# Start-up of a fused convolution and gated-MLP kernel: unbroken TensorE warm-up, held weight requests, one scaling moved to GpSimd

## Chip, cores, metric

One core of one Trainium2 chip. The metric is the device time in microseconds (us) of one execution, the median of several. A profile is one more execution, taken with the hardware profiler; its span is about 1.7 us shorter than the device time of the same execution.

## The reference

```python
def _attn_ref(x, weight):                  # x (8, 4096, 192), weight (8 heads, 7 taps)
    w = softmax of weight over the taps
    x_pad = six zero tokens before each sequence
    out = for each token, head: sum over 7 taps of w[head, k] * x_pad[token + k]
def _moe_ref(x, w_in, w_out, beta):        # 32768 tokens, w_in (192, 2048), w_out (2048, 192)
    h = x @ w_in
    g = h * (1.0 / (1.0 + np.exp(-beta * h)))
    return g @ w_out
```

## The kernel before

Tokens go through in 32 chunks, each of two times 512 tokens. A chunk is a causal 7-tap convolution (`ct`), then 16 units of `hidden` (six matmuls into PSUM, then one Silu on ScalarE) and, interleaved, the output matmuls of `g` with `w_out`. The prediction calls one row-packed couple of output matmuls a pair, and unit u of chunk s is the step (s, u). A request lands when the last of its DMA engines has reported; the drain is the end of the kernel, when little more than output matmuls is left; the clock is released when TensorE's matmuls, throttled at first, go over to their full pace (here from one every 427 ns to one every 231).

Only the start differs from the steady loop. Chunk 0 is transposed on TensorE, its convolution runs mostly as matmuls with diagonal weights, and everything that the loop needs must arrive meanwhile: x, `w_in` in four parts (each part in two requests from GpSimd, which also cast to bf16), and `w_out` in four parts (from the SP queue, scaled by 1/beta afterwards).

```python
    load_x(x0, 0)                       # SP queue, in this order
    load_x(x1, TOK)
    for i in range(NW - 1):
        load_w_out(i)
    load(2)
    load_w_out(NW - 1)
    load(3)
    ...
    load_w_in(0)                        # GpSimd queue, two requests, at 2.2 us
    ...
    def fill(n, cols=TOK):              # matmuls of zeros that only keep TensorE busy
        for _ in range(n):
            nc.tensor.matmul(
                pf[:, 0, 0:cols], zeros[:, 0:128], zeros[:, 0:cols], start=True, stop=True
            )
    ...
    fill(5)
    pc = in_a()
    pw, pb = pc[:, 0, 0 : K + 1], pc[:, 1, 0:NF]
    nc.tensor.matmul(                   # tap weights onto 128 partitions
        pw, sel.rearrange("i h p -> i (h p)"), e8, start=True, stop=True
    )
    fill(1, 384)
    for b in range(NB):
        cast_rows(nc.vector.tensor_copy, x0b, x0, b)
    ...
    hold = setup.tile([1, 1], BF16)
    nc.gpsimd.tensor_copy(hold, x0b[0:1, 0, 0, 0, 0:1])   # waits for the first cast
    for i in range(1, NW):
        load_w_in(i)                    # the other six requests
    ...
    for b in range(NB):
        transposes(pt, x0b, b)
        nc.scalar.copy(tokens(xt0, b), pt)
        # fills of 256, 384, 384 columns, beta's transpose, 256 columns
    ...
    # chunk 0's convolution: 7 + 7 + 2 matmuls of N=512 ("conv matmuls"), 5 taps on VectorE
    nc.vector.reciprocal(beta_r, beta)
    scale_w_out(0)                      # VectorE
    ...
    CONV1 = {4: (0, 2), 5: (2, 4), 6: (4, 6), 7: (6, K)}  # chunk 1's third on TensorE, by unit
    QUOTA_A = {3: 4, 7: 2}              # output pairs in units up to 7 of chunk 0
```

Of the kernel before, what the change touches and what calls it, by code (L numbers as in the profile page):

```python
# [9 lines left out]
FP32 = mybir.dt.float32  # L10
FP32R = mybir.dt.float32r
BF16 = mybir.dt.bfloat16
# [5 lines left out]
def kernel(  # L18
# [17 lines left out]
    nc = tc.nc  # L36

    B, S, D = x.shape
    H, K = weight.shape
# [5 lines left out]
    TOK = 512  # L45
    NF = F // 128
    PAD = K - 1
    HALO = 16
# [13 lines left out]
    setup = ctx.enter_context(tc.tile_pool(name="setup", bufs=1))  # L62
# [18 lines left out]
    def in_a():  # L81
        return psum_a.tile([128, 2, TOK], FP32, name="pa")
# [20 lines left out]
    def cast(ch, h):  # L103
        if h == 0:
            xbs[ch] = xb_pool.tile([128, NB, NG, 2, DG], BF16, name="xb")
        nc.vector.tensor_copy(  # L106
            xbs[ch][:, :, :, h, :],
            xfs[ch][:, h].rearrange("q b (p c) -> q b c p", c=NG),
        )
# [13 lines left out]
    def xpose(ch):  # L123
        xt = new_xt(ch)
        halo(ch, xts[ch - 1])
        for b in range(NB):
            nc.sync.dma_start_transpose(
                xt[:, :, HALO + b * BLK : HALO + (b + 1) * BLK],
                xbs[ch][:, b].rearrange("q c h p -> q (c h p)"),
            )  # L130


    NW = 4
# [4 lines left out]
    x0b = setup.tile([128, NB, NG, 2, DG], BF16)  # L138
# [11 lines left out]
    e8 = setup.tile([H, K + 1], FP32)  # L150
# [18 lines left out]
    for i in range(NW - 1):  # L169
# [2 lines left out]
    load_w_out(NW - 1)  # L172
    load(3)

    zeros = setup.tile([128, TOK], BF16)
    nc.vector.memset(zeros, 0.0)
    warm = setup.tile([H, 1], FP32)
    nc.vector.memset(warm, 0.0)  # L178
    xt0 = setup.tile([128, NG, HALO + TOK], FP32R)
# [3 lines left out]
    sel = setup.tile([H, 2, DG], FP32)  # L183
# [6 lines left out]
        fill=0.0,  # L190
# [8 lines left out]
        fill=0.0,  # L199
# [7 lines left out]
    def load_w_in(i):  # L207
        cols = slice(i * FW, (i + 1) * FW)
        for r in range(2):
            nc.gpsimd.dma_start(  # L210
                out=w_in_s[r * DG : (r + 1) * DG, :, cols], in_=w_in_v[:, :, cols]
            )

    load_w_in(0)

    nmax = setup.tile([H, 1], FP32)
    nc.vector.reduce_max(nmax, cw8, axis=mybir.AxisListType.X, negate=True)
    nc.scalar.activation(
        e8[:, 0:K], cw8, AF.Exp, bias=nmax, accum_out=e8[:, K : K + 1]
    )  # L220
    nc.scalar.activation(warm, warm, AF.Silu)
    ident_b = setup.tile([128, 128], BF16)
    nc.vector.tensor_copy(ident_b, ident)
    pf = psum_h.tile([128, 2, TOK], FP32, name="ph")

    def fill(n, cols=TOK):
        for _ in range(n):
            nc.tensor.matmul(  # L228
                pf[:, 0, 0:cols], zeros[:, 0:128], zeros[:, 0:cols], start=True, stop=True
            )  # L230

    def cast_rows(copy, xb, x, b):
        copy(  # L233
            xb[:, b].rearrange("q c h p -> q h c p"),
            x[:, b // 2, :, b % 2].rearrange("q h (p c) -> q h c p", c=NG),
        )

    def transposes(pt, xb, b):
        for c in range(NG):
            nc.tensor.transpose(  # L240
                pt[:, c, :], xb[:, b, c].rearrange("q h p -> q (h p)"), ident_b
            )

    def tokens(xt, b):
        t = HALO + (b // 2) * 2 * BLK
        return xt[:, :, t : t + 2 * BLK].rearrange("p c (q b) -> p c b q", b=2)[:, :, b % 2]
# [2 lines left out]
    beta_r = setup.tile([128, NF], FP32)  # L249
    cw = consts.tile([128, K], FP32)  # L250
    rn = setup.tile([128, 1], FP32)

    fill(5)
    pc = in_a()
    pw, pb = pc[:, 0, 0 : K + 1], pc[:, 1, 0:NF]
    nc.tensor.matmul(
        pw, sel.rearrange("i h p -> i (h p)"), e8, start=True, stop=True
    )
    fill(1, 384)
    for b in range(NB):  # L260
        cast_rows(nc.vector.tensor_copy, x0b, x0, b)
    nc.vector.reciprocal(rn, pw[:, K : K + 1])
    nc.vector.tensor_scalar_mul(cw, pw[:, 0:K], rn)

    hold = setup.tile([1, 1], BF16)
    nc.gpsimd.tensor_copy(hold, x0b[0:1, 0, 0, 0, 0:1])
    for i in range(1, NW):
        load_w_in(i)

    diag = setup.tile([128, K, 128], FP32R)  # L270
    xt1 = setup.tile([128, HALO + TOK], FP32R)
# [19 lines left out]
    for b in range(NB):  # L291
        pt = pts[b % 2][:, b // 2, 0 : NG * BLK].rearrange("p (c q) -> p c q", c=NG)
        transposes(pt, x0b, b)
        nc.scalar.copy(tokens(xt0, b), pt)
        if b == 0:
            fill(1, 256)
        elif b == 1:
            fill(1, 384)
    fill(1, 384)
    nc.tensor.transpose(pb, beta_q, ident[0:NF, 0:NF])  # L300
    nc.scalar.copy(beta, pb)
    fill(1, 256)
    for k0, k1 in ((0, 3), (3, K)):
        nc.vector.tensor_tensor(
            diag[:, k0:k1],
# [4 lines left out]

    def scale_w_out(i):
        fcs = slice(i * NQ, (i + 1) * NQ)
        nc.vector.tensor_tensor(  # L313
            w_out_s[:, fcs, :],
            w_out_raw[:, fcs, :],
            beta_r[:, fcs].unsqueeze(2).to_broadcast((128, NQ, D)),
            ALU.mult,
        )
# [28 lines left out]
    nc.vector.tensor_tensor(dst, pv, dst, ALU.add)  # L347
    nc.vector.reciprocal(beta_r, beta)
    scale_w_out(0)


# [25 lines left out]
        nc.vector.tensor_copy(xt1[:, HALO - PAD :], xt[:, 0, HALO - PAD :])  # L377


    CONV1 = {4: (0, 2), 5: (2, 4), 6: (4, 6), 7: (6, K)}  # L380
    conv1_ps = []

    def conv1(u):
        if not conv1_ps:
            new_ct(1)
            conv1_ps.append(in_b())
        pv = conv1_ps[0]
        for k in range(*CONV1[u]):
            for r in range(2):
                diag_tap(k, xt1, pv[:, r, :], slice(r * DG, (r + 1) * DG))  # L390
# [7 lines left out]
    def conv_ops(s, c0):  # L398
        def op(k):
            if s not in cts:  # L400
                new_ct(s)
            o = HALO - PAD + k
            tap(cts[s][:, c0:, :], xts[s][:, c0:, o : o + TOK], k)

        return [lambda k=k: op(k) for k in range(K)]
# [82 lines left out]
    def jobs_of(s):  # L488
        for h in range(2):
            for q in range(0, NB, 2):  # L490
                if s == N_ST - 1 and h == 1 and q == NB - 2:
                    waiting.extend([Job(s, h, q, 1), Job(s, h, q + 1, 1)])
                else:
                    waiting.append(Job(s, h, q, 2))

    def output(s, u, pairs, free):
        for _ in range(pairs):
            for name in free:
                if slots[name] is None and waiting:
                    slots[name] = waiting.popleft()  # L500

            live = [(j.s, j.h, j.q, n) for n, j in slots.items() if j is not None]
            for *_, name in sorted(live):
                job = slots[name]
                if job.ready(s, u):
                    break
            else:
                return
            if job.po is None:
                job.po = place[name]()  # L510
            if job.pair():
                job.leave()
                slots[name] = None

    def rows_of(ch):
        for h in range(2):
            cast(ch, h)
        xpose(ch)


    first_work = {
        4: [None, lambda: scale_w_out(1), None],
        5: [None],
        7: [conv1_evac, lambda: scale_w_out(2), lambda: rows_of(2), None],
        8: [None, lambda: scale_w_out(3)],
        9: [None],
        10: [None],
    }

    QUOTA_A = {3: 4, 7: 2}  # L530
    queue = deque()
    for s in range(N_ST):
        jobs_of(s)
        for u in range(NF):
            if s > 0 or u > 1:
                hidden(s, u)
            elif u == 0:
                phs = [hidden(0, fc, [0]) for fc in range(2)]
                for j in range(1, NG):
                    for fc in range(2):  # L540
                        hidden(0, fc, [j], phs[fc])
                second()
            if s > 0:
                output(s, u, 8 if s < N_ST - 1 else 7, "ab")
            elif u > 7:
                output(s, u, 5 if u < NF - 1 else 8, "ab")
            elif u in QUOTA_A:
                output(s, u, QUOTA_A[u], "a")
            if s == 0:
                if u in CONV1:  # L550
                    conv1(u)
                if u == min(CONV1):
                    queue.extend(conv_ops(1, 1))
                for work in first_work.get(u, []):
                    (work or queue.popleft())()
            else:
                if u % 2 and queue:
                    queue.popleft()()

                if u == 0 and s + 3 < N_CH:  # L560
                    load(s + 3)
                if u < 2 and s + 2 < N_CH:
                    cast(s + 2, u)
                if u == 1 and s + 2 < N_CH:
                    xpose(s + 2)
            if u == 12 and s + 2 < N_CH:
                queue.extend(conv_ops(s + 2, 0))
# [32 lines left out]
```

## Time and profile before

| | before |
|---|---|
| device time, median | 693.09 us (692.62 to 693.2, 3 runs) |
| span of the profiled run | 690.7 us |
| first conv matmul | 7.83 us |
| first `hidden` matmul | 12.88 us |
| first Silu | 14.31 us |
| first Silu of chunk 1 | 32.57 us |

Read such a profile from its end: which chain of work ended last? This is part 4 of the page of the kernel before, by engine; by line its largest entries are `hidden` (L417, 47%) and the output matmuls (L450, 24% into each of two PSUM tiles). L279 is the conv matmul.

```profile
PE 97%; DVE 1%; ACT 1%; issue 0%; ACTq 0%
...
```

TensorE is full from 32 us to the drain, so a change of the start is worth exactly what it shifts the moment when TensorE becomes full, plus the work that is left for the end. The timeline of the kernel before, some lines (start us, duration us, engine, line, operation, output<-inputs, count, and in brackets the idle time before and what ended it):

```profile
7.83 3.04 PE L279 MATMUL ph<-xt,diag 128*128 128x512 f32 x7
...
10.71 1.79 PE L279 MATMUL pb<-xt,diag 128*128 128x512 f32 x7
...
12.88 1.47 PE L417 MATMUL ph<-ct,w_in_s 64*128 64x512 bf16 x12
...
14.31 16.15 ACT L425 ACTIVATE g<-ph,beta 128x1024 bf16<-128x1024 f32 x15
14.45 0.96 DVE L313 TENSOR_TENSOR w_out_s<-w_out_raw,beta_r 128x768 bf16<-128x768 f32 x1 [0.62 <-DMA w_out_raw<-in_moe_w_out_dram]
```

The first group of seven conv matmuls takes 3.04 us and the second 1.79, with the same operands: the TensorE clock is released in between (427 ns from start to start, then 231). The first scaling waits for `w_out`.

The chain of waits of the kernel before, for the window from 0 to 45 us, some lines (start us, duration us, what):

```profile
22.33 0.68 DVE ct L396
23.01 0.01 issue
23.02 0.69 DVE ct L396
23.72 0.03 issue
23.75 0.96 DVE w_out_s L313
24.71 1.20 DVE xb L106 x2
...
30.59 1.29 DVE ct L335
31.88 0.04 issue
31.92 0.61 PE ph L417 x4
```

The last obstacle before the steady loop is VectorE, which finishes chunk 1's taps at 31.88 us. What TensorE waited for in the first 36 us of the kernel before (total us, times, longest):

```profile
PE ph L228 <- DVE warm L178: 1.3, 1, 1.3
PE ph L417 <- ACT g L425: 0.9, 2, 0.7
PE ph L417 <- DVE ct L335: 0.4, 1, 0.4
PE pa L256 <- ACT e L218: 0.2, 1, 0.2
```

### The profile page before, as it was taken

The page shows a single profiled execution, that of the slowest core. Times are in us where ns is not written, and L with a number is a line of the kernel's source. Part 1 is how long each engine was busy: PE and PEld are TensorE (multiplying, and loading weights), DVE is VectorE, ACT ScalarE, POOL GpSimd, SP SyncE. Part 2 cuts the span into 40 slices and gives each one's busy share as a digit, 9 for nine tenths or more (in the row PEclk, how much of TensorE's full clock was granted, in tenths as well). Part 3 has the DMA queues.
Part 4 walks back from the last instruction along what each step waited for, and adds up shares of the span by engine and source line. Part 5 has one row for each costly group of instructions (what it writes and reads, how often), then busy time and mean ns, then how long its engine had stood idle before and what let it go on. Part 6 is the DMA issues. An engine that isn't in the chain of part 4 may idle for free.

```text
span 690.7 us, 24335 instructions
## 1 busy us (share of the span) xinstructions
PE 684.2 (99%) x11311; PEld 518.1 (75%) x11311; DVE 526.6 (76%) x466; ACT 579.1 (84%) x531; POOL 6.8 (1%) x18
## 2 busy tenths in 40 slices
PE   8999999999999999999999999999999999999997
PEld 4677777777777777777777777777777777777776
DVE  6888877797777797777887777887777977777712
ACT  6988888888888888888888888888888888888883
POOL 3000000000000000000000000000000000000000
DMA  9754332344332343332344332443323443322111
GB/s 214 176 117 116 93 104 69 85 116 112 92 104 58 102 116 104 97 95 61 109 116 105 93 83 70 116 116 92 104 56 98 116 106 98 98 60 60 48 37 59
DMA packets 121445, 66.86 MB, mean 97 GB/s; under 512 B 53232, under 2 KB 121344, under 8 KB 121344
## 3 DMA queue, kind: packets, MB, share of 16 engines
q1 hardware_dynamic: 119632, 63.73, 34.7%
q0 software_dynamic: 1664, 1.57, 1.4%
q8 instruction: 88, 1.44, 0.9%
q14 instruction: 13, 0.11, 0.1%
q10 hardware_dynamic: 48, 0.01, 0.0%
HBM read 29.89 MB, written 25.17 MB: 80 GB/s over the span
## 4 chain that ended last, share of the span: by engine, by line
PE 97%; DVE 1%; ACT 1%; issue 0%; ACTq 0%
PE ph L417 47%; PE pa L450 24%; PE pb L450 24%; DVE ct L335 1%; ACT g L425 0%; PE ph L279 0%; ACT x1b L233 0%; DVE w_out_s L313 0%; PE pb L279 0%; PE ph L228 0%; DVE ct L396 0%; DVE xb L106 0%; ACT ct L326 0%; PE pb L240 0%; PE ph L240 0%
## 5 line engine op out<-in xcount | busy, mean ns | idle before, releaser
L425 ACT ACTIVATE g<-ph,beta 128x1024 bf16<-128x1024 f32 x512 | 569.7, 1114 | 95.7 <-PE ph L417 89.6
L450 PEld LDWEIGHTS <-g 64*128 64x128 bf16 x8160 | 367.7, 94 | 106.3 <-ACT g L425 0.7
L417 PE MATMUL ph<-ct,w_in_s 64*128 64x512 bf16 x3072 | 422.8, 376 | 1.3 <-ACT g L425 0.9
L335 DVE SCALAR_TENSOR_TENSOR ct<-xt,cw,ct 128x1536 bf16<-128x1536 bf16 (+2 forms) x190 | 336.6, 1772 | 2.5
L450 PE MATMUL pa<-w_out_s,g 64*128 64x192 bf16 x4112 | 244.2, 243 | 0.6 <-ACT g L425 0.5
L450 PE MATMUL pb<-w_out_s,g 64*128 64x192 bf16 (+1 forms) x4048 | 229.7, 243 | 0.0
L417 PEld LDWEIGHTS <-w_in_s 64*128 64x128 bf16 x3072 | 156.7, 94 | 56.7 <-issue 3.4
L468 DVE TENSOR_REDUCE osb<-pa 128x384 f32<-128x768 f32 x64 | 61.3, 957 | 120.8 <-PE pa L450 119.9
L468 DVE TENSOR_REDUCE osb<-pb 128x384 f32<-128x768 f32 x63 | 60.3, 958 | 28.9 <-PE pb L450 28.8
L106 DVE CAST xb<-xf 128x768 bf16<-128x768 f32 x60 | 40.5, 677 | 0.0
L333 DVE TENSOR_SCALAR ct<-xt,cw 128x1536 bf16<-128x1536 bf16 (+2 forms) x32 | 31.1, 972 | 0.0
L466 ACT COPY osb<-pb 128x192 f32<-128x192 f32 x1 | 0.3, 318 | 6.7 <-PE pb L450 6.7
L228 PE MATMUL ph<-zeros 128*128 128x512 bf16 (+2 forms) x10 | 4.7, 551 | 1.3 <-DVE warm L178 1.3
L210 POOL DMA_DIRECT2D w_in_s<-in_moe_w_in_dram x8 | 5.2, 653 | 0.0
L279 PE MATMUL pb<-xt,diag 64*128 64x512 f32 (+1 forms) x21 | 4.7, 453 | 0.0
L313 DVE TENSOR_TENSOR w_out_s<-w_out_raw,beta_r 128x768 bf16<-128x768 f32 x4 | 3.8, 956 | 0.7 <-DMA w_out_raw<-in_moe_w_out_dram 0.6
L121 DVE COPY xt<-xt 128x18 bf16<-128x18 bf16 x27 | 4.3, 159 | 0.0
L326 ACT CAST ct<-ph 128x512 bf16<-128x512 f32 x1 | 0.6, 586 | 3.3 <-PE ph L279 3.3
L279 PEld LDWEIGHTS pb<-xt,diag 64*128 64x128 f32 (+1 forms) x21 | 2.7, 187 | 0.7
L279 PE MATMUL ph<-xt,diag 128*128 128x512 f32 x7 | 3.0, 603 | 0.1
L233 DVE CAST x0b<-x 128x384 bf16<-128x384 f32 x4 | 1.5, 420 | 2.1 <-DMA x<-in_x_dram 2.1
L228 PEld LDWEIGHTS <-zeros 128*128 128x128 bf16 x10 | 1.2, 133 | 2.1 <-DVE warm L178 1.3
(51 smaller groups left out, 27.7 us busy)
## 6 DMA issues: line engine op xcount, KB each, us to landing
out_dram<-osb SPq DMA_DIRECT2D x127, 192.0 KB, 2.1
xf<-in_x_dram SPq DMA_DIRECT2D x60, 384.0 KB, 4.1
xt<-xb SPq DMA_TRANSPOSE x120, 3.1
x<-in_x_dram SPq DMA_DIRECT2D x4, 384.0 KB, 4.6
w_in_s<-in_moe_w_in_dram POOLq DMA_DIRECT2D x8, 192.0 KB, 9.8
w_out_raw<-in_moe_w_out_dram SPq DMA_DIRECT2D x4, 384.0 KB, 14.6
out_dram<-osb SPq DMA_DIRECT2D x2, 96.0 KB, 1.6
cw<-in_weight_dram ACTq DMA_DIRECT2D x1, 0.2 KB
```

The lines of the kernel that those rows point to most:

```text
L106: nc.vector.tensor_copy(xbs[ch][:, :, :, h, :], xfs[ch][:, h].rearrange("q b (p c) -> q b c p", c=NG),)
L121: nc.vector.tensor_copy(dst, last[:, :, HALO + TOK - PAD :])
L210: nc.gpsimd.dma_start(out=w_in_s[r * DG : (r + 1) * DG, :, cols], in_=w_in_v[:, :, cols])
L228: nc.tensor.matmul(pf[:, 0, 0:cols], zeros[:, 0:128], zeros[:, 0:cols], start=True, stop=True)
L279: nc.tensor.matmul(pv, diag[rows, k, :], xt[rows, o : o + TOK], start=(k == k0), stop=(k == K - 1),)
L313: nc.vector.tensor_tensor(w_out_s[:, fcs, :], w_out_raw[:, fcs, :], beta_r[:, fcs].unsqueeze(2).to_broadcast((128, NQ, D)), ALU.mult,)
L333: nc.vector.tensor_scalar_mul(dst, src, scalar)
L335: nc.vector.scalar_tensor_tensor(out=dst, in0=src, scalar=scalar, in1=dst, op0=ALU.mult, op1=ALU.add)
L417: nc.tensor.matmul(ph[:, h, :], w_in_s[rows, j, fc * 128 : (fc + 1) * 128], cts[s][rows, j, :], start=(j == 0), stop=(j == NG - 1),)
L425: nc.scalar.activation(gs[s][:, fc], ph, AF.Silu, scale=beta[:, fc : fc + 1])
L450: nc.tensor.matmul(self.po[:, r, b * D : (b + 1) * D], g[rows, fc, self.h, q * BLK : (q + 1) * BLK], w_out_s[rows, fc, :], start=(self.don ...
L468: nc.vector.tensor_reduce(dst, self.po[:, :, 0 : nb * D].rearrange("p r n -> p n r"), axis=mybir.AxisListType.X, op=ALU.add,)
```

## The change

The intent: (1) keep TensorE busy with eight unbroken N=512 matmuls until the first transposes, so that the clock is released sooner, and do the tap weights' matmul later, among the transposes; (2) hold `w_in` back with two tiny GpSimd copies as barriers: chunk 0's part until ScalarE's Exp is done, the rest until chunk 0 is transposed, so that x and `w_out` come first; (3) put the first `w_out` scaling on GpSimd; (4) end chunk 1's TensorE part one unit earlier and shift output pairs into chunk 0 (52 instead of 49). Cut to its core:

```diff
-    load_w_in(0)
-
     nmax = setup.tile([H, 1], FP32)
     ...                                              # (Exp of the tap weights -> e8)
     nc.scalar.activation(warm, warm, AF.Silu)
+    hold = setup.tile([1, 2], FP32)
+    nc.gpsimd.tensor_copy(hold[:, 0:1], e8[0:1, K:])
+    load_w_in(0)
@@
-    fill(5)
     pc = in_a()
     pw, pb = pc[:, 0, 0 : K + 1], pc[:, 1, 0:NF]
-    nc.tensor.matmul(pw, sel..., e8, ...)
-    fill(1, 384)
+    fill(8)
     for b in range(NB):
         cast_rows(nc.vector.tensor_copy, x0b, x0, b)
-    (reciprocal, cw)
-    hold = setup.tile([1, 1], BF16)
-    nc.gpsimd.tensor_copy(hold, x0b[0:1, 0, 0, 0, 0:1])
-    for i in range(1, NW):
-        load_w_in(i)
@@ in the loop of transposes
         elif b == 1:
-            fill(1, 384)
-    fill(1, 384)
+            nc.tensor.matmul(pw, sel..., e8, ...)
+            (reciprocal, cw)
+            fill(1, 256)
+        elif b == 2:
+            fill(1, 256)
+    fill(1)
     nc.tensor.transpose(pb, beta_q, ident[0:NF, 0:NF])
+    fill(1)
     nc.scalar.copy(beta, pb)
-    fill(1, 256)
+    nc.gpsimd.tensor_copy(hold[:, 1:2], xt0[0:1, 0, HALO + TOK - 1 :].bitcast(FP32))
+    for i in range(1, NW):
+        load_w_in(i)
@@ scale_w_out(i)
-        nc.vector.tensor_tensor(
+        (nc.vector if i else nc.gpsimd).tensor_tensor(
@@
-    CONV1 = {4: (0, 2), 5: (2, 4), 6: (4, 6), 7: (6, K)}
+    CONV1 = {4: (0, 2), 5: (2, 4), 6: (4, K)}
-        7: [conv1_evac, lambda: scale_w_out(2), lambda: rows_of(2), None],
+        6: [conv1_evac, lambda: scale_w_out(2), lambda: rows_of(2), None],
-    QUOTA_A = {3: 4, 7: 2}
+    QUOTA_A = {4: 2, 7: 5}
-                output(s, u, 5 if u < NF - 1 else 8, "ab")
+                output(s, u, 5 if u < NF - 1 else 10, "ab")
```

Below, "first hold" is the barrier before chunk 0's `w_in`, "second hold" the later barrier before the other six requests.

More of the change, by code (lines that the diff above doesn't have):

```diff
@@ L173 @@
     load(3)
-    zeros = setup.tile([128, TOK], BF16)
+    zeros = setup.tile([128, 128], BF16)
     nc.vector.memset(zeros, 0.0)
@@ L226, in fill @@
     def fill(n, cols=TOK):
+        zc = zeros.unsqueeze(1).to_broadcast((128, cols // 128, 128))
         for _ in range(n):
-            nc.tensor.matmul(
-                pf[:, 0, 0:cols], zeros[:, 0:128], zeros[:, 0:cols], start=True, stop=True
-            )
+            nc.tensor.matmul(pf[:, 0, 0:cols], zeros, zc, start=True, stop=True)
     def cast_rows(copy, xb, x, b):
@@ L251 @@
     rn = setup.tile([128, 1], FP32)
-    fill(5)
     pc = in_a()
     pw, pb = pc[:, 0, 0 : K + 1], pc[:, 1, 0:NF]
-    nc.tensor.matmul(
-        pw, sel.rearrange("i h p -> i (h p)"), e8, start=True, stop=True
-    )
-    fill(1, 384)
+    fill(8)
     for b in range(NB):
         cast_rows(nc.vector.tensor_copy, x0b, x0, b)
-    nc.vector.reciprocal(rn, pw[:, K : K + 1])
-    nc.vector.tensor_scalar_mul(cw, pw[:, 0:K], rn)
-    hold = setup.tile([1, 1], BF16)
-    nc.gpsimd.tensor_copy(hold, x0b[0:1, 0, 0, 0, 0:1])
-    for i in range(1, NW):
-        load_w_in(i)
     diag = setup.tile([128, K, 128], FP32R)
@@ L297 @@
         elif b == 1:
-            fill(1, 384)
-    fill(1, 384)
+            nc.tensor.matmul(
+                pw, sel.rearrange("i h p -> i (h p)"), e8, start=True, stop=True
+            )
+            nc.vector.reciprocal(rn, pw[:, K : K + 1])
+            nc.vector.tensor_scalar_mul(cw, pw[:, 0:K], rn)
+            fill(1, 256)
+        elif b == 2:
+            fill(1, 256)
+    fill(1)
     nc.tensor.transpose(pb, beta_q, ident[0:NF, 0:NF])
+    fill(1)
     nc.scalar.copy(beta, pb)
-    fill(1, 256)
+    nc.gpsimd.tensor_copy(hold[:, 1:2], xt0[0:1, 0, HALO + TOK - 1 :].bitcast(FP32))
+    for i in range(1, NW):
+        load_w_in(i)
     for k0, k1 in ((0, 3), (3, K)):
```

## The prediction

> **What bounds the kernel now.** The chain that ended last is 97% TensorE (page, part 4); from 32 us to the drain no wait separates one matmul from the next, and nothing there changes. Gains must come before 32 us, or from work left for the end.
>
> From the timeline and the chain:
> - The clock is cold until about 10.2 us: N=512 matmuls start 427 ns apart, afterwards 231 ns apart. So the first conv group (L279, 7 matmuls, from 7.83) takes 2.9 us to issue, the second 1.6. The chain runs through that group, then ScalarE (0.59 conv copy, 1.32 x1b, 0.58, 1.32) to the first Silu at 14.31.
> - From there TensorE is nearly full (about 1.06 to 1.12 us per unit), with stalls of 0.75 and 0.18 (PSUM held by Silu), 0.4 near 29 us (the last w_out scaling on VectorE) and about 0.6 at 31.3, where chunk 1 waits for VectorE's last tap; the chain is VectorE from 22.3 to 31.9.
> - DMA: w_in is issued at 2.17 but its first packets move at 5.7, dividing the engines with x1 and w_out until 21 us. w_out part 0 lands at 14.36 (its scaling waits 0.6 us), part 1 at 18.2, when its scaling starts.
>
> **The change.**
> 1. Warm-up: eight N=512 fills, about 1.1 to 4.6 us, without the tap-weight matmul (0.49 us). The Trainium skill ("TensorE: Matmul & The Clock Gate", Part 1) gives a free-running activity window of about 3.4 us; Part 4 says that transposes do not count as busy. This trace agrees so far: fills broken by mixed work did not release the clock. One unbroken window may end the cold phase at 5 to 8 us. The fills after the transposes are longer (512+512 columns for 384+256), costing up to 0.5 us if cold. Warm, conv starts about 7.5 (after ScalarE's copies of xt0), its sixteen matmuls take 3.7 us, and the first Silu moves to about 13.1: -1.2 us. If the clock stays cold to 10 us: about 0.
> 2. w_in held: chunk 0's starts about 1.7 us later, but x1 is then done; I estimate that it lands by 11 us (before 12.0). w_out and the loads of chunk 2 land 1 to 4 us earlier.
> 3. The first scaling leaves VectorE: -0.96 us on its chain. On GpSimd I estimate 1.7 us (skill, "GPSIMD Engine Reference", section 3.1: 2.6 cycles per element with two inputs, 768 elements), off the path.
> 4. conv1 ends one unit earlier, so its evacuation starts earlier. The last tap of chunk 1 ends near 30.2 (before 31.88).
> 5. Chunk 0 takes 52 output pairs instead of 49: three pairs of 82 ns leave the drain, -0.25 us.
>
> **Sum:** chunk 1 starts 1.0 to 1.8 us earlier, plus 0.25. Prediction **691.4 us**, 690.3 to 692.7. Faster by over 2%: 1%; within 2%: 98.5%; slower: 0.5%.
>
> **What would show each step.** Conv matmuls 231 ns apart from the first or second one (step 1). First Silu near 13.1. w_in chunk 0 landed before hidden starts; w_out scalings without DMA waits. GpSimd scaling 1.5 to 2.2 us, ended before the first output matmul. ct of chunk 1 ready near 30.2; waits at 29 and 31.5 us shrunk to under 0.3.
>
> **What would make it wrong.** A window phase that keeps the clock cold into conv (gain about 0.5); w_in for chunk 0 landing after 11.5 us; a GpSimd scaling over 3 us; a new wait for chunk 2's loads before its casts.

## More of the kernel before

The queues of the kernel before from 11 to 14 us (packets, MB, share of the time of 16 engines; q0 carries `w_in`, q1 the SP queue's loads), and after them the time from issue to landing of the eight `w_in` requests:

```profile
q0 software_dynamic: 415, 0.39, 77.2%
q1 hardware_dynamic: 415, 0.31, 40.7%
```

```profile
DMA to landing us min/median/max: 8.3/9.8/13.0
```

The two queues moved the same number of packets, 415 each. The Trainium skill says the same in "DMA: Bandwidth & Descriptors", section "Queues, rings and completion order": each DMA engine takes the queues that have work in turn, packet by packet. This trace agrees from 7 to 19 us: in each microsecond the two counts differ by at most 4 (where `w_in`'s queue held only the rest of one request they were far apart, 188 and 761 from 11 to 14 us in the changed kernel). So `w_in` gets every second packet while `w_out` and x are waiting, however urgent it is.

## The result, and the profile after

694.12 us median (693.69 to 694.41, 4 runs) against 693.0 (692.62 to 693.2, 4 runs): ratio 1.0016, interval 0.9999 to 1.0034. The predicted range, 690.3 to 692.7, does not hold it.

| us | before | changed |
|---|---|---|
| first conv matmul | 7.83 | 8.40 |
| clock released | about 10.4 | about 9.9 |
| second request of chunk 0's `w_in` landed | 12.00 | 15.05 |
| first `hidden` that needs it | 12.88 | 15.09 |
| first Silu | 14.31 | 16.44 |
| first Silu of chunk 1 | 32.57 | 34.77 |
| span | 690.7 | 692.7 |

What TensorE waited for in the first 36 us of the changed kernel (L422 is `hidden` now, L272 the conv matmul, L234 the fills):

```profile
PE ph L422 <- DMA w_in_s<-in_moe_w_in_dram: 1.6, 1, 1.6
PE ph L422 <- ACT g L430: 1.1, 3, 0.7
PE ph L234 <- DVE warm L178: 1.1, 1, 1.1
PE pb L244 <- DVE x0b L237: 0.4, 1, 0.4
```

The first line is new. Its place in the changed kernel's timeline, TensorE and ScalarE lines:

```profile
8.40 2.69 PE L272 MATMUL ph<-xt,diag 128*128 128x512 f32 x7
...
10.93 1.77 PE L272 MATMUL pb<-xt,diag 128*128 128x512 f32 x7
...
13.09 0.39 PE L422 MATMUL ph<-ct,w_in_s 64*128 64x512 bf16 x1
...
15.09 1.25 PE L422 MATMUL ph<-ct,w_in_s 64*128 64x512 bf16 x10 [1.61 <-DMA w_in_s<-in_moe_w_in_dram]
...
16.44 1.11 ACT L430 ACTIVATE g<-ph,beta 128x1024 bf16<-128x1024 f32 x1 [1.83 <-PE ph L422]
```

One matmul goes (it needs the first request's 64 partitions only), then TensorE stands until the second request has landed. The chain of waits of the changed kernel, window 0 to 45 us, runs through a later part of the same weights and names the barrier:

```profile
7.82 0.51 ACT xt L287
8.33 0.05 issue
8.39 0.17 POOL hold L304
8.56 0.57 POOL w_in_s L210
9.13 10.98 DMA w_in_s<-in_moe_w_in_dram
20.11 0.05 issue
20.15 0.69 PE ph L422 x5
```

That is the second hold: part 1 of `w_in`, issued at 8.5 us, landed at 20.11 and held up unit 4 as well. The `w_in` requests' times from issue to landing, as shown of before:

```profile
DMA to landing us min/median/max: 7.5/11.5/14.7
```

Later requests did not land faster: the median is 11.5 us, before 9.8 (9.6 and 9.4 in two later traces of the changed kernel). In the trace's semaphore updates the second request's sixteen DMA engines finished one by one from 11.72 to 13.57 us, and the last only at 15.05, a straggler.

From chunk 1 on the distance between the two traces stays +2.20 us, and the span differs by 1.95: the 0.25 us of three output pairs came back in the drain, as predicted. (Another number of the page looks alarming, and is not: weight-load busy time went up with no change of pace. It is in the last section.)

### The profile page after: what moved, and what is told of

Read it like the earlier page. It is cut to its first block, busy times and chain, and to the rows that moved or that the text cites. A ratio compares the mean times of both kernels' runs of the same rounds, so it can differ in the third digit from the quotient of the medians.

```text
span 692.7 us, 24342 instructions
## 1 busy us (share of the span) xinstructions
PE 684.9 (99%) x11314; PEld 634.6 (92%) x11314; DVE 523.1 (76%) x465; ACT 579.3 (84%) x531; POOL 8.3 (1%) x20
## 4 chain that ended last, share of the span: by engine, by line
PE 97%; DMA 2%; ACT 0%; POOL 0%; DVE 0%; issue 0%
PE ph L422 52%; PE pb L455 22%; PE pa L455 21%; DMA w_in_s<-in_moe_w_in_dram 2%; DMA x<-in_x_dram 1%; PE pb L272 0%; ACT g L430 0%; PE pb L244 0%; PE ph L234 0%; PE ph L244 0%; POOL w_in_s L210 0%; PE pa L291 0%; ACT xt L287 0%; DVE x0b L237 0%; ACT osb L471 0%
## 5 line engine op out<-in xcount | busy, mean ns | idle before, releaser
L455 PEld LDWEIGHTS <-g 64*128 64x128 bf16 x8160 | 445.7, 94 | 28.3 <-ACT g L430 0.7
L422 PE MATMUL ph<-ct,w_in_s 64*128 64x512 bf16 x3072 | 463.5, 376 | 2.8 <-DMA w_in_s<-in_moe_w_in_dram 1.6
L455 PE MATMUL pa<-w_out_s,g 64*128 64x192 bf16 x4112 | 277.3, 243 | 0.5 <-ACT g L430 0.5
L455 PE MATMUL pb<-w_out_s,g 64*128 64x192 bf16 (+1 forms) x4048 | 256.7, 243 | 0.0
L422 PEld LDWEIGHTS <-w_in_s 64*128 64x128 bf16 x3072 | 234.7, 94 | 20.2 <-DMA w_in_s<-in_moe_w_in_dram 2.9
L234 PE MATMUL ph<-zeros 128*128 128x512 bf16 (+1 forms) x13 | 6.1, 578 | 1.1 <-DVE warm L178 1.1
L272 PE MATMUL pb<-xt,diag 64*128 64x512 f32 (+1 forms) x21 | 5.0, 434 | 0.0
L234 PEld LDWEIGHTS <-zeros 128*128 128x128 bf16 x13 | 1.7, 137 | 2.8 <-issue 1.7
L272 PEld LDWEIGHTS pb<-xt,diag 64*128 64x128 f32 (+1 forms) x21 | 3.1, 187 | 0.6
## 6 DMA issues: line engine op xcount, KB each, us to landing
w_in_s<-in_moe_w_in_dram POOLq DMA_DIRECT2D x8, 192.0 KB, 11.5
```

What stands on the lines that cost most here:

```text
L234: nc.tensor.matmul(pf[:, 0, 0:cols], zeros, zc, start=True, stop=True)
L272: nc.tensor.matmul(pv, diag[rows, k, :], xt[rows, o : o + TOK], start=(k == k0), stop=(k == K - 1),)
L422: nc.tensor.matmul(ph[:, h, :], w_in_s[rows, j, fc * 128 : (fc + 1) * 128], cts[s][rows, j, :], start=(j == 0), stop=(j == NG - 1),)
L455: nc.tensor.matmul(self.po[:, r, b * D : (b + 1) * D], g[rows, fc, self.h, q * BLK : (q + 1) * BLK], w_out_s[rows, fc, :], start=(self.don ...
```

## The experiments

Three theories at the start. A: the first hold starts chunk 0's `w_in` too late. B: the second hold puts the issue of six requests into the time when chunk 0's `w_in` is moving, and disturbs its last part. C: the longer warm-up sequence is itself the loss. Each run below is 5 rounds (five or six executions, one profiled), with the kernel before on the same chip; "occasion" numbers say which ran together. Landings are those of the second request of chunk 0's `w_in`; landing and first Silu are read from the one profiled execution of each run, the medians from all of them.

| occasion | run | median us | before us | landing us | first Silu us |
|---|---|---|---|---|---|
| 1 | changed, first measurement | 694.12 | 693.00 | 15.05 | 16.44 |
| 2 | a_w0_free | 691.91 | 692.96 | 13.03 | 14.43 |
| 2 | a_rest_free | 693.08 | 692.96 | 14.22 | 15.61 |
| 2 | b_holds | 693.73 | 692.96 | 13.86 | 15.51 |
| 2 | b_warm | 692.77 | 692.96 | 12.07 | 13.46 |
| 3 | after_again | 692.84 | 693.06 | 14.22 | 15.61 |
| 3 | a_no_holds | 692.15 | 693.06 | 12.43 | 13.83 |
| 3 | a_w0_first | 691.88 | 693.06 | 11.53 | 13.25 |
| 3 | b_pool_quota | 692.34 | 693.06 | 11.88 | 13.28 |
| 4 | a_wout_held | 697.67 | 693.15 | 11.32 | 14.54 |
| 4 | a_w0_first_late_rest | 697.34 | 693.15 | 11.46 | 13.11 |
| 4 | b_pool | 692.56 | 693.15 | 11.62 | 14.63 |
| 4 | pool_quota_w0first | 692.64 | 693.15 | 10.92 | 13.22 |
| 5 | after_third | 692.97 | 692.92 | 13.89 | 15.29 |
| 5 | a_w0_free_same_chip | 692.12 | 692.92 | 12.91 | 14.30 |
| 5 | a_w0_first_no_hold | 693.31 | 692.92 | 11.36 | 13.31 |

All outputs were correct. Differences of under about 0.5 us between occasions should not be read.

### Occasion 2: which part loses

**a_w0_free**, the changed kernel without the first hold:

```diff
+    load_w_in(0)
     nmax = setup.tile([H, 1], FP32)
@@
-    nc.gpsimd.tensor_copy(hold[:, 0:1], e8[0:1, K:])
-    load_w_in(0)
```

> The changed kernel without its first hold: chunk 0's two w_in requests are issued at about 2.2 us as in the kernel before; the second hold stays. Theory A (the first hold starts chunk 0's w_in too late) and theory B (the six later requests are issued while chunk 0's w_in is still moving, and delay its last part) both expect chunk 0's w_in to have landed by about 10.5 us, no wait of TensorE for it, first Silu at 14.3 to 14.5 instead of 16.4, and 691.5 to 692.2 us. Theory C (the longer warm-up sequence is the loss) expects no gain: about 694.

691.91 us, inside the range; C would have had 694. The landing was expected by 10.5 and came at 13.03, so TensorE still waited 1.6 us for it: the conv part was ready at 11.1. The profiled run was the slowest of the five (692.91), so its times stand for a poor draw.

**a_rest_free**, the changed kernel without the second hold:

```diff
     for b in range(NB):
         cast_rows(nc.vector.tensor_copy, x0b, x0, b)
+    nc.gpsimd.tensor_copy(hold[:, 1:2], x0b[0:1, 0, 0, 0, 0:1])
+    for i in range(1, NW):
+        load_w_in(i)
@@
-    nc.gpsimd.tensor_copy(hold[:, 1:2], xt0[0:1, 0, HALO + TOK - 1 :].bitcast(FP32))
-    for i in range(1, NW):
-        load_w_in(i)
```

> The changed kernel without its second hold: the first hold stays, so chunk 0's requests are issued at 3.8 us and the other six follow at once (issue over by about 9.5 us). Theory A expects the loss to stay: second request of chunk 0 lands at 14 us or later, 693.5 to 694.2 us. Theory B expects the straggling last part to go: it lands by about 12.8, first Silu 14.3 to 14.7, 691.7 to 692.5 us.

The landing is still 14.22 and the first Silu 15.61: B's picture fails. The time, 693.08, lies below A's range, so A's size was too large.

**b_holds**, the kernel before plus both holds (edit: the lines of the diff above that concern `hold` and `load_w_in`, and nothing else).

> The kernel before plus the two holds alone. Theories A and B expect the loss here: second request of chunk 0's w_in lands near 15 us, TensorE waits 1.5 to 2 us for it, total 694 to 695 us (more than the changed kernel, which also has three output pairs and one VectorE operation less in the way). Theory C expects no loss: about 693.

693.73 us, 0.8 slower than before: a loss from the holds alone, smaller than expected. The trace itself cannot serve as evidence for the wait: in it the clock stayed cold until 13.05 us, conv ended at about 14.2, and `w_in` (13.86) was no longer late.

**b_warm**, the kernel before plus the warm-up rearrangement (edit: `zeros`, `fill`, and the moves of the tap weights' matmul and the fills).

> The kernel before plus the warm-up rearrangement alone. From the changed kernel's trace (conv starts 0.57 us later, clock released about 0.35 us earlier, first conv group ends 0.23 us later) I expect 693.2, a loss of 0.1 to 0.4 us. Theory C expects 694 or more. What I predicted blind would be a gain of about 1.2 us: 691.8.

692.77 us: no loss (the 693.2 expected was too slow), so C falls; and nearly no gain. Its trace is the most instructive of all, because the warm-up did what was predicted: conv began at 7.51 with a warm clock, and ended about 1.5 us sooner than before. TensorE's waits (first 36 us of b_warm), and the timeline lines behind them:

```profile
...
PE pa L450 <- DVE xt L370: 1.0, 1, 1.0
PE ph L417 <- ACT g L425: 0.9, 2, 0.7
PE ph L417 <- DVE ct L335: 0.4, 1, 0.4
PE ph L417 <- DMA w_in_s<-in_moe_w_in_dram: 0.3, 1, 0.3
```

```profile
12.12 1.47 PE L417 MATMUL ph<-ct,w_in_s 64*128 64x512 bf16 x11 [0.33 <-DMA w_in_s<-in_moe_w_in_dram]
...
14.54 0.96 DVE L313 TENSOR_TENSOR w_out_s<-w_out_raw,beta_r 128x768 bf16<-128x768 f32 x1 [2.15 <-DMA w_out_raw<-in_moe_w_out_dram]
...
17.41 0.50 PE L450 MATMUL pa<-w_out_s,g 64*128 64x192 bf16 x8 [0.96 <-DVE xt L370]
```

First Silu 13.46, 0.85 us ahead of before. Then VectorE waits 2.15 us for `w_out` (landed at 14.4 in both kernels), starts chunk 1's copies no sooner than before, and TensorE waits 0.96 us for them. By unit 4 the lead is gone. A faster start only ran into the next transfer.

### Occasion 3: the size of the loss, and the other parts

**after_again**, the changed kernel unedited.

> The changed kernel once more, on this chip beside the others: is its loss the same here, and does chunk 0's second w_in request land late again (15.05 us in its first trace)? Theory A (first hold: late) expects it at 13.5 to 15.5 us and 693.7 to 694.3 us. If the 15.05 was one bad draw, 693.0 or less.

692.84 us (692.75 to 693.62), although the request landed at 14.22. The first measurement was a worse draw by 1.3 us. The traces show where: clock released at about 9.9 us there and 5.8 here, landing 15.05 and 14.22, first Silu of chunk 1 at 34.77 and 33.42.

**a_no_holds**, the changed kernel with both holds put back as before (edits of a_w0_free and a_rest_free together).

> The changed kernel with both holds put back as in the kernel before; warm-up, scaling on GpSimd, conv1 and output shares as changed. Theory A: chunk 0's w_in lands near 12.0, first Silu near 13.4 if the clock is released by 8 us, and since the first scaling no longer sits on VectorE, the 0.96 us wait of TensorE at 17 us (seen with the warm-up alone) goes. VectorE then has to wait for w_out part 1 at 18.2 instead. Expected 691.8 to 692.4 us. If the second hold is what helps, it is above the 691.9 of the kernel without the first hold.

692.15 us, in the range. On the same chip it is 0.7 us faster than the changed kernel.

**a_w0_first**, a_w0_free with the two requests as GpSimd's first work:

```diff
+    load_w_in(0)                    # (with its definition moved up)
     sel = setup.tile([H, 2, DG], FP32)
     nc.gpsimd.memset(sel, 1.0)
@@
-    nc.gpsimd.tensor_copy(hold[:, 0:1], e8[0:1, K:])
-    load_w_in(0)
```

> The changed kernel without its first hold, and chunk 0's two w_in requests issued as GpSimd's first work (0.8 us instead of 2.2); second hold kept. Theory A: the start of the transfer follows the issue by about 3.5 to 4 us, so its last part lands 0.7 to 1.4 us earlier than in the kernel without the first hold (13.03), first Silu 13.2 to 13.8, 690.9 to 691.6 us. If the transfer is set by the bytes ahead of it and not by its issue, it lands no earlier and the time is again 691.9.

691.88 us (691.53 to 692.03), ratio 0.998, interval 0.9967 to 0.9992: faster than the kernel before, by little. (Of all runs only this one, a_no_holds and b_pool_quota have an interval that ends below 1.) Issue 1.3 us, landing 11.53 (1.5 earlier than in a_w0_free). The landing and the first Silu came as expected, the total did not: 691.88 lies above 690.9 to 691.6 and is the 691.9 that was expected if nothing came of it. By medians the earlier issue gained nothing over a_w0_free (691.91, another occasion); their traces, 31.88 and 33.28 us at the first Silu of chunk 1, compare this kernel's fastest execution with that one's slowest. TensorE's waits in the first 36 us:

```profile
PE ph L422 <- ACT g L430: 1.1, 3, 0.8
PE ph L234 <- DVE warm L178: 1.1, 1, 1.1
PE pb L244 <- DVE x0b L237: 0.4, 1, 0.4
PE ph L422 <- DVE ct L340: 0.2, 1, 0.2
PE ph L422 <- DMA w_in_s<-in_moe_w_in_dram: 0.2, 1, 0.2
```

**b_pool_quota**, the kernel before plus parts 3 and 4 of the change (edit: the last five changes of the diff).

> The kernel before plus the scaling on GpSimd, conv1 one unit earlier and the new output shares, without warm-up and holds. My sum of the changed kernel's parts needs 0.2 to 0.7 us of gain here (three pairs of 82 ns, and the 1.0 us of waits at 29 and 31.3 us partly gone): 692.3 to 692.8. A loss would mean that GpSimd's scaling or the shares cost something themselves.

692.34 us, in the range. Its trace, of the fastest of the five, had an early clock release with the old warm-up (about 7.6 us).

### Occasion 4: why the request is late

**a_wout_held**, the changed kernel with the SP queue's loads after x kept back:

```diff
-    for i in range(NW - 1):
-        load_w_out(i)
-    load(2)
-    load_w_out(NW - 1)
-    load(3)
@@ after ScalarE's copy of chunk 0's second ct (c == NG - 2)
+            nc.scalar.copy(w_out_raw[0:1, 0, 0:1], cts[0][0:1, c, 0:1])
+            for i in range(NW - 1):
+                load_w_out(i)
+            load(2)
+            load_w_out(NW - 1)
+            load(3)
```

> The changed kernel with the w_out loads and chunk 2's loads kept back until ScalarE has written chunk 0's second ct (about 11.3 us), so that from 7.8 us chunk 0's w_in has the DMA engines to itself. Theory A1 (w_in is late because it takes turns with w_out, packet by packet): its second request lands at 10.5 to 12.3 instead of 14.2 to 15.05, TensorE waits for it at most 0.5 us, first Silu 13.2 to 13.8. Theory B (the six later requests' issue disturbs it): still 13.5 or later. The total says little here, as w_out and chunk 2 now come some 4 us late: 692 to 695.

With the same issue time as in the changed kernel (3.77 us), the landing came at 11.32 instead of 13.9 to 15.05, and TensorE did not wait for it. Time from issue to landing of the eight requests, and the timeline at `hidden` (L424 here):

```profile
DMA to landing us min/median/max: 4.5/6.7/8.3
```

```profile
12.34 0.62 PE L267 MATMUL pa<-xt,diag 128*128 128x512 f32 x2
12.88 1.47 PE L424 MATMUL ph<-ct,w_in_s 64*128 64x512 bf16 x12
```

The median fell to 6.7 us, from 9.4 to 11.5 in the three traces of the changed kernel, while GpSimd was issuing the six others as before (8.2 to 11.9 us). So what delays chunk 0's `w_in` is the SP queue's traffic beside it (one trace against three, and 2.6 to 3.7 us between them). First Silu 14.54 missed the expected 13.2 to 13.8, because the clock was released only at about 9.8 us in this run. The total, 697.67, lies above the expected range. In the profiled execution (695.85 us, mean granted clock 1.000) `w_out` arrives so late that TensorE waits 3.4 us for the scaling. Four of the six executions took 697.66 to 698.47 us, with a mean granted clock of 0.995 to 0.997; so about 2 us of the median go with a lower clock that the trace does not contain. The kernel is a probe, not a proposal.

**a_w0_first_late_rest**, a_w0_first with the other six requests held until ScalarE's first `ct` (edit: the second hold copies from `cts[0][0:1, 0, 0:1]` after that copy).

> The kernel with chunk 0's w_in issued first and no first hold, with the other six requests held until ScalarE's first ct (about 9.2 us) instead of xt0 (7.5). Theory B: without issue between 7.5 and 9.2 us, chunk 0's second request lands at 9.3 to 10.3 instead of 11.53. Theory A1: it lands at 11 to 12 as before, as w_out is still in its way. Total about 691.7 to 692.3, as part 1 of w_in comes later.

Landing 11.46 against 11.53: no difference, B falls for good. The total, 697.34, misses the expectation by 5 us. Part 1 of `w_in` came at 17.75 and 20.66 us, and TensorE waited 4.0 us for it. That is not all: in this trace the granted clock was back at half from 17.86 to 24.68 us, with `hidden` matmuls up to 647 ns long where 388 is the longest in a_w0_first, and all five executions have a mean granted clock of 0.994 or 0.995. So the loss is waits and a throttled clock together; no run separates them. The six requests may not come much later than the second hold has them.

**b_pool**, the kernel before with only the first scaling on GpSimd (edit: one line).

> The kernel before with only the first w_out scaling on GpSimd. If this is what the 0.7 us gain of scaling plus conv1 plus shares came from: 692.4 to 692.6. If the shares and conv1 are: 692.8 to 693.2. GpSimd's operation should again take 1.47 us and, as it needs w_out at 14.4, end by 16, with the first output pairs (unit 3 in this kernel, about 17.3) not waiting for it.

692.56 us, the first of the two outcomes; so most of the 0.7 us of b_pool_quota may be the scaling, though 0.6 us is hardly more than the spread of occasions and the interval, 0.998 to 1.0004, holds 1. It took 1.467 us there, 14.32 to 15.79, against 0.957 on VectorE, and no output matmul waited for it.

**pool_quota_w0first**, b_pool_quota with chunk 0's `w_in` issued first.

> The kernel before plus scaling on GpSimd, conv1, shares, and chunk 0's w_in issued first; old warm-up and old hold of the rest. Against the same with the new warm-up (691.88) it tells what the new warm-up is worth once w_in is in time: if the clock release matters there, 692.1 to 692.7 with a wide spread over the runs; if not, 691.7 to 692.0.

692.64 us with a narrow spread (692.39 to 692.84). I had overlooked that it differs from a_w0_first in the second hold too, so it does not measure the warm-up. Inconclusive for that question.

### Occasion 5: side by side

**after_third**, the changed kernel unedited; **a_w0_free_same_chip**, the same edit as a_w0_free; **a_w0_first_no_hold**, a_w0_first with the other six requests held only by the first cast, as in the kernel before.

> The changed kernel, third time. Theory A: chunk 0's second w_in request lands between 13.8 and 15.1 us, TensorE waits for it 1.5 us or more in all, 692.8 to 694.2 us; a median over 0.5 us above the run without the first hold on the same chip.

> The changed kernel without its first hold, beside the changed kernel on the same chip. Theory A: 0.5 to 2 us faster than it, about 691.9; w_in lands by 13.1. If both are equal within 0.3 us, the first hold is not the loss and the first measurement was a bad draw.

> Chunk 0's w_in issued as GpSimd's first work, the rest held only as in the kernel before; warm-up, scaling, conv1 and shares as changed. If the second hold helps by letting w_out part 1 and chunk 2 in earlier: 692.2 or more (it was 691.88 with it), VectorE's last tap of chunk 1 at 32 us instead of 31.2. If the second hold gives nothing: 691.5 to 691.9.

All three came out as theory A and the second hold's use had them. 692.97 and 692.12 us on one chip: the first hold costs 0.85 us (single executions overlap, 692.38 to 693.64 and 691.76 to 692.95; in occasion 2, a_rest_free with the first hold and a_w0_free without it, where the second hold differs too, are 1.2 us apart). a_w0_first_no_hold came to 693.31, above the 691.88 with the second hold (another occasion). The second hold earns its place once chunk 0's part is early, and GpSimd's scaling shows how. First a_w0_first_no_hold, then a_w0_first (timelines, GpSimd's scaling):

```profile
16.01 1.47 POOL L319 TENSOR_TENSOR w_out_s<-w_out_raw,beta_r 128x768 bf16<-128x768 f32 x1 [6.94 <-DMA w_out_raw<-in_moe_w_out_dram]
```

```profile
13.55 1.47 POOL L318 TENSOR_TENSOR w_out_s<-w_out_raw,beta_r 128x768 bf16<-128x768 f32 x1 [2.27 <-DMA w_out_raw<-in_moe_w_out_dram]
```

Without the hold `w_out`'s first part lands 2.5 us later, VectorE waits 3.7 us for its second part (with it 0.4), and its last tap of chunk 1 ends at 32.67 instead of 31.18.

I had overlooked one pair: a_w0_first_no_hold is a_no_holds with chunk 0's requests issued first. They landed 1.1 us earlier (11.36 against 12.43), and the median was 1.2 us worse (693.31 against 692.15, another occasion). Why is not shown.

## Why the prediction was wrong

**What bounds the kernel: right.** After chunk 1's start every trace keeps its distance to the other.

**Step 1, warm-up: right in mechanism and mostly in size, worth little alone.** The release of the clock can be read from the start-to-start times of equal matmuls and from the trace's record of the granted clock. In the twelve traces with the new warm-up it came by 6.8 us in ten and at 9.8 to 9.9 in two; in the five with the old one between about 7.6 and 13.1. The first trace of the changed kernel was one of the two late ones. The -1.2 us to the first Silu did not come in the changed kernel, for a reason that the prediction named only as a risk: b_warm gained 0.85 us there and gave all of it back at the next transfers. That a phase of a free-running window decides the draw is what the Trainium skill says ("TensorE: Matmul & The Clock Gate", Part 1); the runs show only the spread.

**Step 2, the holds: this is the step that failed.** The prediction put it: "I estimate that it lands by 11 us (before 12.0)". It landed at 15.05, 14.22 and 13.89 us in three traces of the changed kernel. Two terms were too small. With the issue 1.7 us later and the 3.5 us to the first packet that the trace of before showed (2.2 to 5.7), the packets would start at 7.4, and 11 leaves 3.6 us for the two requests. (This sum is worked out afterwards; the prediction gives only its result.) In fact the first packet moved at 8.1 to 8.2 us, and the requests then needed 5.8 to 6.9 us beside `w_out`. The trace of before had shown that too: from 5.67 to 12.00, 6.3 us. I had put the length of that transfer down to x1, which would now be out of the way, and not to `w_out`. a_wout_held shows the cause: with that traffic removed the same requests begin to move at 6.47 and land at 11.32. That is still 4.85 us from first packet to landing, more than the 3.6 us: the estimate was too short even without `w_out` beside it.

The price of the first hold, measured side by side, is 0.85 us. The rest of the missing gain is only argued: conv, ended by about 11.7 us with an early clock, could not be used before `w_in` was there, but with `w_in` there at 11.53 (a_w0_first) the median was no better than with 13.03 (a_w0_free). Why one DMA engine straggled by another 1.5 us in the first trace stays open, as does why the start of `w_in`'s packets itself takes longer beside the SP queue (2.7 us after the issue in a_wout_held).

The second half of the step was right: the first three parts of `w_out` landed about 5 us earlier (14.36 to 9.21, 18.21 to 13.08, and by its semaphore's updates 21.34 to 16.42), and no scaling waited for them in the changed kernel, and a_w0_first against a_w0_first_no_hold shows the second hold useful.

**Step 3, scaling on GpSimd: right for GpSimd.** Estimated 1.7 us, took 1.47, and no output matmul waited for it in b_pool; alone 0.6 us faster than before, not clear of noise. The 0.96 us on VectorE's chain does not show in b_pool's trace: there its second scaling started at 17.86, when `w_out`'s second part had landed (17.84), and its last tap ended at 32.04, no sooner than the 31.87 of the kernel before (the clock was released late in that run, at 11.3 us).

**Step 4, conv1 earlier and VectorE's last tap at 30.2: not reached.** It ended at 32.0 to 33.7 in the changed kernel, being carried along by step 2; in b_pool_quota at 31.09, and in the kernel with the lowest median, a_w0_first, at 31.18. So 30.2 was missed by 0.9 us also where `w_in` was in time. In a_w0_first VectorE began chunk 1's copies at 13.26 (15.33 in the kernel before) and lost part of that lead in new waits: 0.36 us for `w_out`'s second part and 0.80 us for chunk 2's loads, which the prediction had named as a risk.

**Step 5, three pairs: right.** The distance of the traces shrinks by 0.25 us between chunk 1 and the end (2.20 to 1.95; in after_third 0.54 to 0.29).

**The sum.** Predicted -1.7 us. Over three occasions the changed kernel was +1.1, -0.2 and +0.05 us against before, by medians: about no change, with the first occasion as a poor draw. (The other two medians, 692.84 and 692.97, lie above the range too.) With the first hold taken out and chunk 0's `w_in` issued at once, the same change gives -1.2 us (691.88), which lies in the range that was predicted for it as it stood.

## What to carry to other kernels

When DMA queues share engines packet by packet, a request that is needed first does not catch up after it was held back: here 1.6 us of hold came back as 0.9 to 2.1 us in its landing (13.89 to 15.05 with the first hold, 12.91 and 13.03 without). So hold the requests that are needed last, and not by much more than here (a_w0_first_late_rest lost 5 us), and leave the urgent one alone. Issuing it still earlier moved its landing forward by 1.0 to 1.5 us in three pairs of kernels and the median in none (691.88 against 691.91, 693.31 against 692.15, 692.64 against 692.34; each pair of different occasions); what took the gain up is shown only in part (step 4). A transfer that ends just in time is a limit in waiting: before counting a compute gain, look up when each operand of the next step lands, and stop the count there. Where start-up contains a draw (clock release, DMA order), judge a change of one microsecond by several occasions and by the traces, not by one median; and look at the granted clock of every execution, since the profiled one may be another draw than the median.

## What the Trainium skill lacked or had wrong

- "TensorE: Matmul & The Clock Gate", Part 1, says that the transition point varies by about 500 ns from run to run (and elsewhere in that part that one kernel had 6, 11 or 14 cold matmuls). Here the same 3.4 us block of unbroken N=512 matmuls was followed by a release anywhere from 4.0 to 9.9 us in twelve traces; in the old arrangement from about 7.6 to 13.1 in five.
- The same page, Part 4, says that the full clock does not engage for transposes. After a release, this kernel's N=128 transposes started 55 to 56 ns apart, before it 107 (a_w0_free, and the first trace of the changed kernel): as far as these are the transposes that the page means, they do run at the released clock.
- "DMA: Bandwidth & Descriptors", first table, gives about 1 us of first-byte latency for requests from GpSimd. With the SP queue busy, the first packet moved 3.0 to 4.4 us after the issue began (1.3 to 4.26 us, 3.77 to 8.21), and 2.7 us with that queue idle for part of the time (3.77 to 6.47).
- The same page, "Queues, rings and completion order", agrees with the runs on taking turns by packet (415 and 415 packets in 3 us), but has no consequence for the reader: a transfer of two requests of 192 KB took 5.5 to 7.2 us from first packet to landing beside another queue (sixteen traces), and 4.85 us with most of that queue's traffic held back (a_wout_held).
- "Trainium Kernel Development and Optimization" calls weight-load busy time a good measure of how near a kernel is to its limit. Here it rose from 518.1 to 634.6 us with the same number of loads of the steady loop, 94 ns each, and no change of pace (both traces keep 20.92 us per chunk): the sum of the loads is the same, so fewer of them overlapped, probably because the two row halves of a couple ran out of step after the late request. (It is 508.8 and 545.6 us in the other two traces of the changed kernel.) The busy lines of the two pages, before and then changed:

```profile
PE 684.2 (99%) x11311; PEld 518.1 (75%) x11311; DVE 526.6 (76%) x466; ACT 579.1 (84%) x531; POOL 6.8 (1%) x18
```

```profile
PE 684.9 (99%) x11314; PEld 634.6 (92%) x11314; DVE 523.1 (76%) x465; ACT 579.3 (84%) x531; POOL 8.3 (1%) x20
```

- "GPSIMD Engine Reference", section 3.1, would make the scaling 1.66 us by my estimate (2.6 cycles per element, 768 elements); it took 1.466 to 1.468 us in every run but one (1.479).
